# Moving small operations off VectorE in a fused attention and gated-unit kernel

## The chip, the cores and the metric

The kernel runs on one core of one Trainium2 chip. The metric is the device time of one execution in microseconds (us), lower is better. Before the change it is 220.66 us, the median of three runs (220.55 to 221.03). Times are compared by the ratio to the kernel before. Kernels are compared only within the same rounds. Line numbers such as L645 are lines of the kernel in question, so the same statement has another number before and after the change.

## The reference

The input x (2048 tokens of 512 channels, bfloat16) is layer-normalised to xn. Two branches of xn are added to x.

```python
qkv = xn @ wqkv                                   # 32 heads of 16
pq, pk = q @ w_phi, k @ w_phi                     # per head, 16x16
phi = concat([softmax(p), softmax(-p)])           # for q and for k: 32 features a head
kv  = sum_s phi_k[s] v[s]^T ;  z = sum_s phi_k[s]
A   = (phi_q kv) / (phi_q z + 1e-6) @ wo
B   = ((xn @ w_gate) * (xn @ w_up)) @ w_down      # width 1792
out = x + A + B
```

## The kernel before

All work is recorded as steps with their reads and writes. A small planner in the kernel's program orders the steps on each engine by assumed costs and issues them in that order, with semaphores between engines. TensorE has six PSUM banks in a ring for everything but two accumulators. Its matmuls are nearly all of the kernel's time; in the notes below a matmul of "512 columns" is one whose moving operand has 512 columns.

The parts that the change touches:

```python
# head: loads. SP is SyncE's queue, ACT is ScalarE's
load_x(SP, 0, 1)
load_x(ACT, 1, 1)                 # the second tile of 128 tokens, "x1"
load_gu(SP, "g", 0, 2)
load_gu(ACT, "u", 0, 2)
# ... cut ...
sc.chain("st0 ag0 st1 ag1 nm0 nm1 xe0d xe1d st2 ...")   # order forced on VectorE

def LN(ts, turn=True, ...):       # st = statistics, ag = their aggregate
    # ... bn_stats, bn_aggr on VectorE; Ln, Exp on ScalarE give rstd ...
    dve(tensor_scalar(out=xn, in0=x, scalar1=mean, scalar2=rstd, op0=subtract, op1=mult))
    # tiles 4 to 15 (turn=True) are then transposed by DMA, tiles 0 to 3 by TensorE

def even_up(ev, sm, rc, ratio, name, t):          # once per tile for k, once for q
    dve(tensor_tensor(out=ratio, in0=smv[:, :, 0], in1=rc, op=mult))      # 128x32, float32
    pool(tensor_tensor(out=ev1, in0=ev1, in1=ratio.broadcast, op=mult))   # GpSimd

def V(t):
    dve(tensor_tensor(out=o1, in0=psum_v, in1=rs.broadcast, op=mult))
    dve(tensor_copy(out=ve[:, :, 64:68], in_=rp_))                        # the cast, 128x32

def U(ft, sg):                    # a gated unit: two PSUM banks
    g = act(copy of bank bg)
    h = dve(tensor_tensor(out=h, in0=bank(bu), in1=g, op=mult))           # L710: frees the bank

def TSUMS():                      # sums of w_down blocks, on GpSimd, 128x1792 elements each
    sums(POOL, T1, ...); sums(POOL, T2, ...); sums(POOL, T4, ...); sums(POOL, T3, ...)
# ... cut: matmuls of the down projection, posts on VectorE, stores ...
```

The softmax here doesn't subtract the row's maximum and nothing guards it: scores larger than these inputs give would overflow.

## Time and profile before

| | before |
|---|---|
| time, median of 3 | 220.66 us |
| span of the profiled run | 219.2 us |
| busy: TensorE, VectorE, ScalarE, GpSimd | 211.1, 174.1, 80.4, 112.4 us |
| matmuls in the program, records of them in the trace | 1634, 1612 |

TensorE is busy 96% of the span. The question is what its few idle moments are. The list of waits of the kernel before, cut to matmuls and weight loads (engine, line, releaser, total us, times, longest):

```profile
PE ps L449 <- DVE arena L710: 1.6, 1, 1.6
PEld ps L449 <- DVE arena L574: 1.5, 2, 1.1
PEld ps L449 <- ACT arena L421: 1.0, 2, 0.7
PEld ps L449 <- DMA arena<-in_B_w_up_dram: 0.6, 1, 0.6
```

One wait of 1.6 us stands out; the others shown are at the head, but for 0.3 us. The table of stretches of the kernel before shows where it is (busy us of each engine, number of instructions in brackets):

```profile
core 0: us, PE busy (x) PEld busy (x) DVE busy (x) ACT busy (x) POOL busy (x), PEclk, DMA share, GB/s
40.00:45.00 5.00, 4.95 (x31) 2.39 (x31) 5.00 (x13) 2.24 (x6) 1.06 (x1) 1.00 0.98 317
...
60.00:65.00 5.00, 3.36 (x34) 2.04 (x34) 5.00 (x8) 3.28 (x7) 4.88 (x3) 1.00 0.00 0
65.00:70.00 5.00, 5.00 (x31) 2.41 (x30) 5.00 (x7) 1.62 (x4) 4.87 (x3) 1.00 0.00 0
```

VectorE has no free moment there (5.00 of 5 us), yet the number of its instructions falls from 13 to 7 per stretch once GpSimd is full too. The timeline at that place shows why (start, duration, engine, line, operation):

```profile
61.94 3.57 POOL L788 TENSOR_TENSOR arena<-arena 128x1792 bf16<-128x1792 bf16 x1
61.98 0.68 DVE L710 TENSOR_TENSOR arena<-ps,arena 128x512 bf16<-128x512 f32 x1
...
62.94 3.33 PE L449 MATMUL ps<-arena 128*128 128x512 bf16 x14 [1.64 <-DVE arena L710]
63.04 0.62 DVE L668 TENSOR_TENSOR arena<-ps,arena 128x512 bf16<-128x512 f32 x1
63.58 1.98 DVE L645 TENSOR_TENSOR arena<-arena 128x32 f32<-128x32 f32 x1
```

The ratio product L645 has 32 elements per partition and lasts 1.98 us. It ends at 65.56, when GpSimd's subtraction L788 ends (65.51). The product at 61.98, with one input in PSUM, runs under the same subtraction in its usual 0.68 us. The groups of the kernel before (busy us, mean ns of one; then idle time before):

```profile
L645 DVE TENSOR_TENSOR arena<-arena 128x32 f32<-128x32 f32 x32 | 17.3, 542 | 0.0
L671 DVE CAST arena<-arena 128x32 bf16<-128x32 f32 x16 | 6.7, 421 | 0.0
L574 DVE TENSOR_SCALAR arena<-arena 128x512 bf16<-128x512 bf16 x16 | 6.4, 429 | 0.3 <-ACT arena L421 0.3
```

The same shows all through this trace. Of the 32 ratio products 13 start while GpSimd runs a subtraction (L788). Each of these ends 0.045 to 0.049 us after that subtraction, and they last 0.28 to 1.98 us; the other 19 last 0.16 to 0.19 us, with a median of 0.18. Of the 16 casts (L671) six start with more than 0.1 us of a product or a subtraction of GpSimd (L647, L788) to go. They end 0.03 to 0.04 us after one and last 0.56 to 1.90 us; the other ten last 0.17. Two of the 16 normalisings (L574) are longer too, 0.77 and 0.67 us against 0.30 to 0.41, and end 0.15 us after a GpSimd instruction. The other groups of VectorE show none of it: the median of L710 is 675 ns for the 14 that start during a GpSimd product or subtraction and 673 for the 14 that meet none, and the reductions L639 take 1.22 us in both cases. Below, an instruction that ends in this way just behind one of GpSimd is said to wait it out.

### The profile page before, as it was taken

The page shows a single profiled execution, that of the slowest core. Times are in us where ns is not written, and L with a number is a line of the kernel's source. Part 1 is how long each engine was busy: PE and PEld are TensorE (multiplying, and loading weights), DVE is VectorE, ACT ScalarE, POOL GpSimd, SP SyncE. Part 2 cuts the span into 40 slices and gives each one's busy share as a digit, 9 for nine tenths or more (in the row PEclk, how much of TensorE's full clock was granted, in tenths as well). Part 3 has the DMA queues.
Part 4 walks back from the last instruction along what each step waited for, and adds up shares of the span by engine and source line. Part 5 has one row for each costly group of instructions (what it writes and reads, how often), then busy time and mean ns, then how long its engine had stood idle before and what let it go on. Part 6 is the DMA issues. An engine that isn't in the chain of part 4 may idle for free.

```text
span 219.2 us, 4090 instructions
## 1 busy us (share of the span) xinstructions
PE 211.1 (96%) x1612; PEld 139.7 (64%) x1634; DVE 174.1 (79%) x370; ACT 80.4 (37%) x173; POOL 112.4 (51%) x88
## 2 busy tenths in 40 slices
PE   8989999999979999999999999999999999999994
PEld 2775444444534454455565667888888888888983
DVE  3856999999999999699994748766877599667652
ACT  3647554354463334536432322333142332341000
POOL 5300031129899896256717535838658567311630
PEclk9999999999999999999999999999999999999998
DMA  6999872762200000002573040341453504535221
GB/s 187 312 253 377 193 145 51 238 174 90 51 0 0 3 0 0 0 4 48 96 98 74 30 89 3 84 110 41 95 60 72 99 24 99 95 72 89 57 75 49
DMA packets 48019, 19.95 MB, mean 91 GB/s; under 512 B 36848, under 2 KB 48000, under 8 KB 48000
## 3 DMA queue, kind: packets, MB, share of 16 engines
q1 hardware_dynamic: 47296, 19.28, 38.5%
q10 hardware_dynamic: 672, 0.39, 0.6%
q8 instruction: 13, 0.21, 0.4%
q14 instruction: 6, 0.05, 0.1%
q0 software_dynamic: 32, 0.02, 0.1%
HBM read 8.67 MB, written 2.10 MB: 49 GB/s over the span
## 4 chain that ended last, share of the span: by engine, by line
PE 73%; DVE 16%; DMA 5%; issue 4%; ACT 1%; SPq 1%
PE ps L449 73%; DVE arena L639 3%; DMA arena<-in_B_w_up_dram 3%; DVE arena L710 2%; DVE arena L566 2%; DMA arena<-arena 2%; DVE arena L657 2%; DVE arena L574 2%; DVE arena L668 2%; DVE arena L671 1%; DVE arena L645 1%; ACT arena L421 1%; SPq L172 1%; DVE arena L822 0%; DVE arena L568 0%
## 5 line engine op out<-in xcount | busy, mean ns | idle before, releaser
L449 PE MATMUL ps<-arena 128*128 128x256 bf16 (+3 forms) x1602 | 206.7, 289 | 4.1 <-DVE arena L710 1.6
L449 PEld LDWEIGHTS ps<-arena 128*128 128x128 bf16 x1624 | 138.3, 98 | 73.1 <-DVE arena L710 1.6
L421 ACT ACTIVATE arena<-ps 128x512 bf16<-128x512 f32 (+2 forms) x152 | 75.3, 535 | 117.2 <-PE ps L449 116.2
L788 POOL TENSOR_TENSOR arena<-arena 128x896 bf16<-128x896 bf16 (+1 forms) x36 | 74.4, 2070 | 38.8 <-PE ps L449 28.3
L647 POOL TENSOR_TENSOR arena<-arena 128x512 bf16<-128x512 bf16 x32 | 33.9, 1059 | 54.8 <-DVE arena L645 53.3
L639 DVE TENSOR_REDUCE arena<-arena 128x64 f32<-128x1024 bf16 x32 | 38.7, 1210 | 8.8 <-ACT arena L421 8.8
L822 DVE TENSOR_TENSOR arena<-ps,arena 128x256 f32<-128x256 f32 (+1 forms) x64 | 26.2, 415 | 11.7 <-PE ps L449 11.3
L710 DVE TENSOR_TENSOR arena<-ps,arena 128x512 bf16<-128x512 f32 x38 | 25.4, 669 | 5.9 <-PE ps L449 5.7
L721 DVE TENSOR_TENSOR arena<-ps,arena 128x256 bf16<-128x256 f32 x34 | 14.0, 412 | 10.3 <-ACT arena L421 10.3
L645 DVE TENSOR_TENSOR arena<-arena 128x32 f32<-128x32 f32 x32 | 17.3, 542 | 0.0
L566 DVE BATCH_NORM_STATS2 arena<-arena 128x6 f32<-128x512 bf16 x16 | 10.3, 671 | 2.5 <-DMA arena<-in_A_x_dram 2.5
L769 DVE TENSOR_TENSOR arena<-ps,arena 128x512 bf16<-128x512 f32 x16 | 11.0, 687 | 0.4
L668 DVE TENSOR_TENSOR arena<-ps,arena 128x512 bf16<-128x512 f32 x16 | 10.2, 637 | 0.4 <-PE ps L449 0.4
L657 DVE RECIPROCAL arena<-arena 128x64 f32<-128x64 f32 x16 | 8.6, 537 | 0.0
L421 ACT ACTIVATE arena<-arena 128x2 f32<-128x2 f32 (+1 forms) x20 | 5.0, 252 | 4.7 <-DVE arena L568 4.4
L671 DVE CAST arena<-arena 128x32 bf16<-128x32 f32 x16 | 6.7, 421 | 0.0
L574 DVE TENSOR_SCALAR arena<-arena 128x512 bf16<-128x512 bf16 x16 | 6.4, 429 | 0.3 <-ACT arena L421 0.3
L765 DVE RECIPROCAL arena<-arena 128x32 f32<-128x32 f32 x16 | 5.6, 347 | 0.3
L745 DVE RECIPROCAL arena<-arena 128x32 f32<-128x32 f32 x16 | 5.5, 344 | 0.1
L887 PE MATMUL ps<-const-bfloat16-1.0 128*128 128x512 bf16 x10 | 4.4, 629 | 0.8 <-PEq L1032 0.8
L549 POOL TENSOR_TENSOR arena<-arena 128x128 bf16<-128x128 bf16 x4 | 1.7, 426 | 3.4 <-DMA arena<-in_A_w_phi_dram 3.4
L887 PEld LDWEIGHTS ps<-const-bfloat16-1.0 128*128 128x128 bf16 x10 | 1.4, 142 | 3.0 <-issue 3.0
(17 smaller groups left out, 13.8 us busy)
## 6 DMA issues: line engine op xcount, KB each, us to landing
out_dram<-arena SPq DMA_DIRECT2D x15, 128.0 KB, 1.8
arena<-in_B_w_down_dram SPq DMA_DIRECT2D x1, 1792.0 KB, 7.9
arena<-in_A_x_dram SPq DMA_DIRECT2D x3, 512.0 KB, 10.4
arena<-in_B_w_gate_dram SPq DMA_DIRECT2D x1, 768.0 KB, 8.0
arena<-in_B_w_up_dram SPq DMA_DIRECT2D x1, 768.0 KB, 9.5
arena<-arena SPq DMA_TRANSPOSE x44, 3.0
arena<-in_B_w_gate_dram SPq DMA_DIRECT2D x2, 256.0 KB, 4.6
arena<-in_B_w_gate_dram SPq DMA_DIRECT2D x1, 512.0 KB, 7.1
```

The source lines that it names most:

```text
L421: return e.activation(out=out_ap, in_=in_ap, func=func, scale=scale, **kw)
L449: ins = e.matmul(o, lhsT=l, rhs=r, start=s, stop=p, skip_group_check=True)
L566: dve(lambda e, t=t: e.bn_stats(stats_v[:, t, :], x_tile(t)), [x_tile(t)], [stats_v[:, t, :]], cost=560.0, name=f"st{t}", win=win)
L639: dve(lambda e: e.tensor_reduce(out=sm, in_=Et.rearrange("p (h f) -> p h f", f=16), axis=AX.X, op=ALU.add), [Et], [sm], cost=1130.0, name= ...
L645: dve(lambda e: e.tensor_tensor(out=ratio, in0=smv[:, :, 0], in1=rc, op=ALU.mult), [sm, rc], [ratio], cost=100.0, name=f"{name}q{t}")
L647: pool(lambda e: e.tensor_tensor(out=ev[:, :, 1, :], in0=ev[:, :, 1, :], in1=ratio[:, :, None].to_broadcast([128, H, 16]), op=ALU.mult), [ ...
L657: dve(lambda e: e.reciprocal(out=rs, in_=sm), [sm], [rs], cost=500.0, name=f"kc{t}")
L668: dve(lambda e: e.tensor_tensor(out=o1, in0=src, in1=rp_[:, :, :, None].to_broadcast([128, 8, 4, 16]), op=ALU.mult), [src, rs_v[:, t % 4, ...
L710: dve(lambda e: e.tensor_tensor(out=h, in0=bank(bu), in1=g, op=ALU.mult), [bank(bu), g], [h], name=f"h{ft}.{sg}")
L721: dve(lambda e: e.tensor_tensor(out=h, in0=bank(b, 256, 256), in1=g, op=ALU.mult), [bank(b, 256, 256), g], [h], name=f"h{ft}.{s_lo}")
L788: fn = lambda e: e.tensor_tensor(out=out_, in0=a_, in1=b_, op=op)
L822: dve(lambda e: e.tensor_tensor(out=out_, in0=in_ps, in1=in_sb, op=ALU.add), [in_ps, in_sb], [out_], cost=328.0, name=f"{name}.{p}")
```

## The change

The intent is to take off VectorE what was seen to wait out GpSimd's instructions: the ratio goes to GpSimd, the normalising of tiles 4 to 15 and the casts to ScalarE. Around this, the loads of the head are re-ordered, w_phi is loaded through SyncE's queue, GpSimd's long sums are cut in quarters, tile 0 is normalised in two halves, two of the first 256-column units are cut into four of 128 columns, and the last stores are cut in quarters.

```diff
-    load_x(ACT, 1, 1)
+    load_x(SP, 1, 1)
     load_gu(SP, "g", 0, 2)
-    load_gu(ACT, "u", 0, 2)
+    load_gu(ACT, "u", 0, 2, after=identity)
@@ LN: tiles 4 to 15
-            dve(tensor_scalar(out=xn_tile(t), in0=x_tile(t), scalar1=mean, scalar2=rstd, ...))
+                pool(tensor_scalar(out=nb, in0=mean, scalar1=rstd, scalar2=-1.0, op0=mult, op1=mult))
+                act_op(xn_tile(t), x_tile(t), func=Identity, scale=rstd, bias=nb)
@@ even_up
-        dve(lambda e: e.tensor_tensor(out=ratio, in0=smv[:, :, 0], in1=rc, op=ALU.mult), ...)
+        pool(lambda e: e.tensor_tensor(out=ratio, in0=smv[:, :, 0], in1=rc, op=ALU.mult), ...)
@@ V
-        dve(lambda e: e.tensor_copy(out=ve[:, :, 64:68], in_=rp_), ...)
+        sc.step(ACT, lambda e: e.activation(out=ve[:, :, 64:68], in_=rp_, func=ACTF.Copy), ...)
@@ TSUMS: each of the four sums
+            for lo, hi in ((0, 2), (2, 4), (4, 6), (6, HF)):
+                sums(POOL, o_[:, lo:hi], a_[:, lo:hi], b_[:, lo:hi], ALU.subtract, ...)
@@ last pair of tiles: three quarter stores by SP as soon as each is ready, and
+                store(t2, 256, 256, ACT)
@@ head
-    for ft in range(4): U2(ft, 256)
+    U1(0, 2); U1(1, 2); U1(0, 3); U1(1, 3); U2(2, 256); U2(3, 256)
-    sc.chain("st0 ag0 st1 ag1 nm0 nm1 xe0d ...")
+    sc.chain("st0 ag0 st1 ag1 nm0.0 nm0.1 nm1 xe0d ...")
(cut: the moved w_phi load, allocation of nb, helpers)
```

More of the change, by code (lines that the diff above doesn't have):

```diff
@@ L388, in _build @@
     alloc("eps", 2 * 2)
+    alloc("nb", 2 * NT)
     alloc("sums", 2 * 4 * 64)
@@ L505, in load_sq @@
         return sc.dma(eng, v, src, nbytes, writes=[v], name=name, after=after)
+    identity = pool(lambda e: e.memset(ident, 0.0), [], [ident], 150.0, name="c")
     load_x(SP, 0, 1)
-    load_x(ACT, 1, 1)
+    load_x(SP, 1, 1)
     load_gu(SP, "g", 0, 2)
-    load_gu(ACT, "u", 0, 2)
+    load_gu(ACT, "u", 0, 2, after=identity)
     sc.step(ACT, lambda e: e.preload_act_table_set("natural_log_exp_and_others"), cost=1300.0, lat=0.0, name="tbl")
@@ L516, in _build @@
     load_gu(SP, "u", 4, 4)
+    sc.dma(SP, wphi_v, bass.AP(tensor=A_w_phi.tensor, offset=A_w_phi.offset, ap=[[16, 128], [2048, NQ], [1, 16]]),
+           16384, writes=[wphi_v], name="wphi")
     load_wT(1)
@@ L523, in _build @@
     load_x(SP, 12, 4)
-    sc.chain("x0 wg0 x2 wg2 wu2 wg4 wu4 wT1 wv x4 wg8 wu8 x8 x12")
-    sc.chain("x1 wu0 tbl")
-    def ms_fn(e):
-        return e.memset(ident, 0.0)
-    pool(ms_fn, [], [ident], 150.0, name="c")
+    sc.chain("x0 x1 wg0 x2 wg2 wu2 wg4 wu4 wphi wT1 wv x4 wg8 wu8 x8 x12")
+    sc.chain("wu0 tbl")
     def af_fn(e):
@@ L534, in _build @@
     pool(af_fn, [ident], [ident], 250.0, name="c")
-    sc.dma(POOL, wphi_v, bass.AP(tensor=A_w_phi.tensor, offset=A_w_phi.offset, ap=[[16, 128], [2048, NQ], [1, 16]]),
-           16384, writes=[wphi_v], name="wphi")
     def band(ap, nb, w, blk):
@@ L558, in _build @@
     eps_f = sbf("eps", 0, 1)
+    nb_v = sbf("nb", 0, NT)
     dve(lambda e: e.memset(eps_f, 1e-5), [], [eps_f], cost=70.0, name="eps")
@@ L562, in xn_tile, with LN @@
         return sbv("xn", (t % 4) * 512, 512)
-    def LN(ts, turn=True, win=60.0, aevac=False):
+    def LN(ts, turn=True, win=60.0, halves=((0, 512),)):
         for t in ts:
@@ L573, in LN @@
         for t in ts:
-            dve(lambda e, t=t: e.tensor_scalar(out=xn_tile(t), in0=x_tile(t), scalar1=mv_v[:, t, 0:1],
-                                               scalar2=rstd_v[:, t:t + 1], op0=ALU.subtract, op1=ALU.mult),
-                [x_tile(t), mv_v[:, t, :], rstd_v[:, t:t + 1]], [xn_tile(t)], cost=325.0, name=f"nm{t}", win=win)
             if turn:
+                pool(lambda e, t=t: e.tensor_scalar(out=nb_v[:, t:t + 1], in0=mv_v[:, t, 0:1],
+                                                    scalar1=rstd_v[:, t:t + 1], scalar2=-1.0, op0=ALU.mult,
+                                                    op1=ALU.mult),
+                     [mv_v[:, t, :], rstd_v[:, t:t + 1]], [nb_v[:, t:t + 1]], 150.0, name=f"nb{t}")
+                act_op(xn_tile(t), x_tile(t), func=ACTF.Identity, scale=rstd_v[:, t:t + 1], bias=nb_v[:, t:t + 1],
+                       name=f"nm{t}")
                 o = xnT_v[:, :, t * 128:(t + 1) * 128]
                 sc.dma(SP, o, xn_tile(t), 131072, turn=True, reads=[xn_tile(t)], writes=[o], name=f"xT{t}")
+                continue
+            for lo, n in halves:
+                dve(lambda e, t=t, lo=lo, n=n: e.tensor_scalar(out=xn_tile(t)[:, lo:lo + n], in0=x_tile(t)[:, lo:lo + n],
+                                                               scalar1=mv_v[:, t, 0:1], scalar2=rstd_v[:, t:t + 1],
+                                                               op0=ALU.subtract, op1=ALU.mult),
+                    [x_tile(t), mv_v[:, t, :], rstd_v[:, t:t + 1]], [xn_tile(t)[:, lo:lo + n]],
+                    cost=65.0 + 0.51 * n, name=f"nm{t}" if n == 512 else f"nm{t}.{lo // 256}", win=win)
     rp = [0]
@@ L644, in even_up @@
         smv = sm.rearrange("p (h s) -> p h s", s=2)
-        dve(lambda e: e.tensor_tensor(out=ratio, in0=smv[:, :, 0], in1=rc, op=ALU.mult), [sm, rc], [ratio],
-            cost=100.0, name=f"{name}q{t}")
+        pool(lambda e: e.tensor_tensor(out=ratio, in0=smv[:, :, 0], in1=rc, op=ALU.mult), [sm, rc], [ratio],
+             180.0, name=f"{name}q{t}")
         pool(lambda e: e.tensor_tensor(out=ev[:, :, 1, :], in0=ev[:, :, 1, :],
@@ L670, in V @@
             cost=600.0, name=f"vs{t}")
-        dve(lambda e: e.tensor_copy(out=ve[:, :, 64:68], in_=rp_), [rs_v[:, t % 4, :]],
-            [ve[:, c, 64:68] for c in range(8)], cost=90.0, name=f"vz{t}")
+        sc.step(ACT, lambda e: e.activation(out=ve[:, :, 64:68], in_=rp_, func=ACTF.Copy), reads=[rs_v[:, t % 4, :]],
+                writes=[ve[:, c, 64:68] for c in range(8)], cost=140.0, name=f"vz{t}")
     def kvb(c):
@@ L784, in parts @@
     def parts(v):
-        return [v[:, k, :] for k in range(HF)]
+        return [v[:, k, :] for k in range(v.shape[1])]
     def sums(eng, out_, a_, b_, op, name):
@@ L795, in TSUMS @@
     def TSUMS():
-        sums(POOL, T1, B12, B11, ALU.subtract, "T1")
-        sums(POOL, T2, B22, T1, ALU.subtract, "T2")
-        sums(POOL, T4, B21, T2, ALU.subtract, "T4")
-        sums(POOL, T3, B22, B12, ALU.subtract, "T3")
+        for n, (o_, a_, b_) in enumerate(((T1, B12, B11), (T2, B22, T1), (T4, B21, T2), (T3, B22, B12))):
+            for lo, hi in ((0, 2), (2, 4), (4, 6), (6, HF)):
+                sums(POOL, o_[:, lo:hi], a_[:, lo:hi], b_[:, lo:hi], ALU.subtract, f"Ts{n}.{lo}")
     def hA(half, t):
@@ L823, in post, with store @@
             cost=328.0, name=f"{name}.{p}")
-    def store(t, lo, n):
+    def store(t, lo, n, eng=SP):
         o = sbv("ostg", (t % 4) * 512 + lo, n)
-        sc.dma(SP, out_flat[t * 128:(t + 1) * 128, lo:lo + n], o, n * 256, is_out=True, reads=[o],
+        sc.dma(eng, out_flat[t * 128:(t + 1) * 128, lo:lo + n], o, n * 256, is_out=True, reads=[o],
                name=f"out{t}.{lo}")
@@ L861, in s5 @@
             post(p, o(t2, 0), pb, t21, "c21")
+            if p == NT // 2 - 1:
+                store(t2, 0, 256)
         def s6():
@@ L865, in s6 @@
             post(p, o(t1, 1), pa, x(t1, 1), "c12")
+            if p == NT // 2 - 1:
+                store(t1, 256, 256)
         def s7():
@@ L869, in s7 @@
             post(p, o(t1, 0), pb, t11, "c11")
-            store(t1, 0, 512)
+            store(t1, 0, 256 if p == NT // 2 - 1 else 512)
         def s8():
@@ L876, in s8 @@
             if p == NT // 2 - 1:
-                store(t2, 0, 256)
-                store(t2, 256, 256)
+                store(t2, 256, 256, ACT)
             else:
@@ L891, in _build @@
     WARM(10)
-    LN([0], turn=False)
+    LN([0], turn=False, halves=((0, 256), (256, 256)))
     T(0, split=True)
@@ L905, in _build @@
     U2(3, 0)
-    for ft in range(4):
-        U2(ft, 256)
-    sc.chain("st0 ag0 st1 ag1 nm0 nm1 xe0d xe1d st2 ag2 st3 ag3 nm2 h0t0 nm3 xe2d h1t0 xe3d h0t1 h1t1")
-    sc.chain("ln0 rs0 ln1 rs1 xe0a xe1a ge0t0 ln2 rs2 ge1t0 ln3 rs3 ge0t1 xe2a ge1t1 xe3a")
+    U1(0, 2)
+    U1(1, 2)
+    U1(0, 3)
+    U1(1, 3)
+    U2(2, 256)
+    U2(3, 256)
+    sc.chain("st0 ag0 st1 ag1 nm0.0 nm0.1 nm1 xe0d xe1d st2 ag2 h0t0 st3 nm2 ag3 xe2d nm3 h1t0 h0t1 xe3d h1t1")
+    sc.chain("ln0 rs0 ln1 rs1 xe0a xe1a ge0t0 ge1t0 ln2 rs2 ge0t1 ln3 rs3 ge1t1 xe2a xe3a")
     units = [(U, ft, 0) for ft in range(4, NF)] + [(U, ft, sg) for sg in (1, 2) for ft in range(NF)]
```

## The prediction

> **What bounds the kernel now.** TensorE. The page has it busy 96% of the span. [...]I find 203.3 us of necessary time in 215.2 us between first and last matmul. The 11.8 us of excess are: about 2 us in the ten warm-up matmuls; four waits at the head (0.64 us before the first transpose, 0.36 at 5.8, 0.57 at 8.4 for the second w_up slice, landing at 8.93, and 0.69 at 11.1 for the evacuation of a transpose); some eighteen evenly spaced gaps of 0.22 us that answer to no wait; 0.30 at 115.8 for a transposing DMA; and one real stall, 1.81 us at 61.1, for VectorE (the product at L710 that frees a PSUM bank). After the last matmul come about 3.1 us of adds and stores.
>
> VectorE (79%) is full only from 24 to 80 us (window table: 5.00 of every 5 us). The chain of waits runs through it from 23 to 63 us, but that is backlog: TensorE keeps its full rate there, fed from six PSUM banks, until the backlog reaches it at 61.
>
> **What the change does.** The ratio product (L645) is 128x32; it takes 0.18 us when free, 542 ns on average, 1.98 us at 63.6 under a GpSimd subtraction. The cast at L671 averages 421 ns, free 0.17. [...] Taken off VectorE: 17.3 us of ratios, 6.7 of casts, 12 of 16 normalisings at 0.43 = 5.2; about 29 us, so 174 falls to about 145.
> Added: [...] GpSimd: 32 ratios and 12 small biases, estimate 0.2 us each: 112 to about 118.
>
> **On the critical path.** Per K tile VectorE's work falls from about 5.6 us to about 4.2, against about 4.5 of TensorE's: no backlog, so the stall at 61 goes (-1.8). After 63 us TensorE hardly waits for anything, so the other freed VectorE time is worth nothing. Head: the 0.69 us wait should nearly vanish (128-column units stand after the transposes: -0.5); the wait for w_up stays, perhaps +0.1 to +0.3 later, because x1 is now issued ahead of it by SyncE. Tail: three quarter stores leave earlier, the last through ScalarE's queue: -0.3. New stall: at 21 to 27 us ScalarE is already 4.0 of 5 us busy and gets four normalisings; expected 0.2. Sum: 220.7 - 1.8 - 0.5 - 0.3 + 0.2 + 0.2 = 218.4 us.
>
> **Range.** 217.2 to 219.6. Faster by over 2% (under 216.3): 4%; within 2%: 95%; slower: 1%.
>
> **Right if:** L710's stall at 61 is gone; VectorE near 145 us and no longer 5.00 of 5 in 25-60; matmul groups unchanged; w_up still ends a wait near 9 us; the chain runs through TensorE.
>
> **Wrong if:** ScalarE's normalisings delay the exponentials so that TensorE waits for a bank at 22-30 us; the ratio on GpSimd queues behind subtractions and delays query transposes, so that TensorE waits after 80 us; the w_up slice lands much later; or the 0.22 us gaps change.

The term of -1.8 us needs only the lengths that the trace shows. The 203.3 us of necessary time come out of the trace as well, to 0.5 us: with the median spacings in it (216, 109, 56 and 33 ns for 512, 256, 128 and 68 columns) the recorded matmuls take 203.8 us. The 0.2 us for a small GpSimd instruction is an estimate that names no figure.

## More of the kernel before

The head of the kernel before, in the timeline:

```profile
0.80 0.41 ACTq L172 DMA_DIRECT2D arena<-in_A_x_dram  x1
...
4.25 0.66 DVE L566 BATCH_NORM_STATS2 arena<-arena 128x6 f32<-128x512 bf16 x1
...
5.05 0.38 DVE L574 TENSOR_SCALAR arena<-arena 128x512 bf16<-128x512 bf16 x1
...
5.49 3.09 PE L449 MATMUL ps<-arena 128*128 128x128 bf16 x40 [0.22 <-DVE arena L574]
```

Ten warm-up matmuls occupy TensorE from 0.84 to 5.26 us; the first transpose starts at 5.49. The statistics of x1 (the line at 4.25) follow those of x0 without a wait for their load. In what follows, "the clock" is the one that TensorE is granted: in this trace 512-column matmuls start 427 ns apart (median) before 6.48 us, which is called half rate here, and 216 ns apart after it, the full rate.

## The result, and the profile after

The changed kernel takes 219.53 us (median of 4 runs, 219.14 to 219.87) against 220.75 us for the kernel before in the same comparison. The ratio of the two is 0.9943 with a 95% interval of 0.9922 to 0.9964. All ratios here are the mean time of one kernel's runs over the mean of the other's in the same rounds, so not quite the ratio of the medians quoted beside them. The range of the prediction holds the time, but the gain is half of the forecast 2.2 us. A second look at the same kernel (a_again below) gave a ratio of 0.9879 (0.9838 to 0.9921), a gain of about 2.7 us, so the size of the gain depends on the executions that one happens to draw; the head, below, is the likely reason.

The groups of the kernel after that answer to those of before:

```profile
L653 POOL TENSOR_TENSOR arena<-arena 128x32 f32<-128x32 f32 x32 | 8.3, 261 | 32.3 <-DVE arena L753 18.7
L679 ACT ACTIVATE arena<-arena 128x32 bf16<-128x32 f32 x16 | 3.7, 231 | 9.3 <-DVE arena L665 9.3
L422 ACT ACTIVATE arena<-arena 128x512 bf16<-128x512 bf16 x12 | 9.1, 805 | 1.4 <-POOL arena L573 1.4
```

Two stretches of the kernel after, the one where a new wait was feared and the one where TensorE had waited:

```profile
core 0: us, PE busy (x) PEld busy (x) DVE busy (x) ACT busy (x) POOL busy (x), PEclk, DMA share, GB/s
25.00:30.00 5.00, 5.00 (x25) 2.25 (x23) 3.54 (x8) 5.00 (x13) 0.94 (x4) 1.00 0.39 79
...
60.00:65.00 5.00, 5.00 (x43) 2.91 (x42) 2.79 (x5) 3.51 (x8) 5.00 (x6) 1.00 0.00 0
```

VectorE fell from 5.00 to 2.79 us in the stretch from 60 to 65, and TensorE's wait is gone. ScalarE is full from 25 to 30, but TensorE does not wait for it. In the chain that ended last, TensorE's share rose from 73% to 95% of the span (before, then after):

```profile
PE 73%; DVE 16%; DMA 5%; issue 4%; ACT 1%; SPq 1%
PE 95%; DMA 2%; DVE 1%; ACT 0%; SPq 0%; issue 0%
```

The head got worse. The timeline of the kernel after:

```profile
0.81 0.86 SPq L172 DMA_DIRECT2D arena<-in_A_x_dram  x2
...
2.97 0.69 DVE L564 BATCH_NORM_STATS2 arena<-arena 128x6 f32<-128x512 bf16 x1 [2.04 <-DMA arena<-in_A_x_dram]
...
4.84 0.69 DVE L564 BATCH_NORM_STATS2 arena<-arena 128x6 f32<-128x512 bf16 x1 [0.96 <-DMA arena<-in_A_x_dram]
...
5.66 1.10 DVE L583 TENSOR_SCALAR arena<-arena 128x256 bf16<-128x256 bf16 x3
...
6.04 11.19 PE L450 MATMUL ps<-arena 128*128 128x128 bf16 x114 [0.78 <-DVE arena L583]
```

x0 lands earlier than before (2.95 instead of 3.40), but x1, now second in SyncE's queue, lands only at 4.81 instead of 3.61. Its issue starts just 0.45 us later (1.25 instead of 0.80). What also changed is the order: ScalarE's queue, freed of x1, now issues the first slice of w_up (256 KB, twice x1) at 1.03, ahead of x1, where it was issued behind it before (1.24). That slice lands at 4.60, and x1 0.2 us after it. The two transfers were issued by different engines and yet ran at the same time: the packets of x1 lie at 3.3 to 4.3 us, among those of w_up (2.3 to 4.1). How much of the delay is the issue and how much is w_up was not separated. VectorE's forced order puts the statistics of x1 ahead of the normalising of x0, so everything waits for x1, and the first transpose starts 0.55 us later. That is not all. The stretches of one us just behind it, before:

```profile
7.00:8.00 1.00, 1.00 (x22) 1.00 (x20) 0.97 (x4) 0.29 (x2) 0.67 (x3) 1.00 1.15 324
```

and after:

```profile
7.00:8.00 1.00, 1.00 (x12) 0.96 (x11) 0.69 (x3) 0.38 (x1) 0.00 (x0) 1.00 1.13 306
8.00:9.00 1.00, 1.00 (x12) 1.00 (x11) 0.96 (x4) 0.28 (x1) 0.00 (x0) 1.00 1.09 354
```

The same 128-column matmuls run at half the rate: 12 instead of 22 begin in a us. In the trace they start 107 ns apart (median) in place of 56. The trace's clock events have the clock come up at 6.48 us before and at 10.07 us after. The page's column PEclk says 1.00 all along: it knows nothing ahead of the first event.

The difference of the two profiled spans is 1.65 us (219.23 and 217.58). Where it came from can be read off at fixed places of TensorE's program. The table gives the start (us) of the same group of 68-column matmuls, with the same columns ahead of it in both programs, and the two ends:

| place | before | after | difference | step |
|---|---|---|---|---|
| second group | 43.43 | 44.54 | +1.11 | head: +1.11 |
| seventh group | 68.04 | 67.43 | -0.61 | wait at 61: -1.72 |
| seventeenth group | 105.79 | 105.18 | -0.61 | 0 |
| twentieth group | 121.28 | 120.23 | -1.05 | small waits, one for a transposing DMA: -0.44 |
| last group | 206.89 | 205.84 | -1.05 | 0 |
| end of the span | 219.23 | 217.58 | -1.65 | stores: -0.60 |

This compares one execution of each. The other traces show how far two of the steps can be trusted. In the seven traces with the head of before, the second group starts between 42.97 (b_onein) and 44.03 us (b_rvz). From the seventeenth to the twentieth group the traces of all kernels take 15.05 to 15.60 us; c_x1warm, which has all of the freeing, takes 15.46, and b_onein, which moves nothing off VectorE, 15.05. So the -0.44 is not shown to come from the change. The step at 61 us is clear of this: from the sixth to the seventh group it is 8.05 us before and 8.07 in b_tail, and 6.32 or 6.33 in every trace with all of VectorE's freeing.

### The profile page after: what moved, and what is told of

It reads as the page before. It is cut to its first block, busy times and chain, and to the rows that moved or that the text cites. A ratio compares the mean times of both kernels' runs of the same rounds, so it can differ in the third digit from the quotient of the medians.

```text
span 217.6 us, 4184 instructions
## 1 busy us (share of the span) xinstructions
PE 213.3 (98%) x1650; PEld 141.4 (65%) x1650; DVE 152.7 (70%) x313; ACT 91.2 (42%) x203; POOL 123.3 (57%) x143
## 4 chain that ended last, share of the span: by engine, by line
PE 95%; DMA 2%; DVE 1%; ACT 0%; SPq 0%; issue 0%
PE ps L450 95%; DMA arena<-in_A_x_dram 2%; DVE arena L829 0%; DVE arena L564 0%; ACT arena L422 0%; DVE arena L583 0%; SPq L172 0%; DVE arena L566 0%
## 5 line engine op out<-in xcount | busy, mean ns | idle before, releaser
L450 PE MATMUL ps<-arena 128*128 128x256 bf16 (+3 forms) x1640 | 208.8, 291 | 0.9 <-DVE arena L583 0.8
L450 PEld LDWEIGHTS ps<-arena 128*128 128x128 bf16 x1640 | 140.0, 99 | 70.4 <-DVE arena L583 2.3
L796 POOL TENSOR_TENSOR arena<-arena 128x896 bf16<-128x896 bf16 (+2 forms) x48 | 76.4, 1600 | 25.8 <-PE ps L450 16.7
L829 DVE TENSOR_TENSOR arena<-ps,arena 128x256 f32<-128x256 f32 (+1 forms) x64 | 26.4, 414 | 11.8 <-PE ps L450 11.6
L653 POOL TENSOR_TENSOR arena<-arena 128x32 f32<-128x32 f32 x32 | 8.3, 261 | 32.3 <-DVE arena L753 18.7
L729 DVE TENSOR_TENSOR arena<-ps,arena 128x256 bf16<-128x256 f32 x32 | 13.2, 414 | 11.7 <-ACT arena L422 11.7
L422 ACT ACTIVATE arena<-arena 128x2 f32<-128x2 f32 (+2 forms) x32 | 14.0, 457 | 4.5 <-DVE arena L566 2.7
L573 POOL TENSOR_SCALAR arena<-arena 128x1 f32<-128x1 f32 x12 | 3.0, 265 | 17.0 <-ACT arena L422 17.0
L679 ACT ACTIVATE arena<-arena 128x32 bf16<-128x32 f32 x16 | 3.7, 231 | 9.3 <-DVE arena L665 9.3
```

What stands on the lines that cost most here:

```text
L422: return e.activation(out=out_ap, in_=in_ap, func=func, scale=scale, **kw)
L450: ins = e.matmul(o, lhsT=l, rhs=r, start=s, stop=p, skip_group_check=True)
L729: dve(lambda e: e.tensor_tensor(out=h, in0=bank(b, 256, 256), in1=g, op=ALU.mult), [bank(b, 256, 256), g], [h], name=f"h{ft}.{s_lo}")
L796: fn = lambda e: e.tensor_tensor(out=out_, in0=a_, in1=b_, op=op)
L829: dve(lambda e: e.tensor_tensor(out=out_, in0=in_ps, in1=in_sb, op=ALU.add), [in_ps, in_sb], [out_], cost=328.0, name=f"{name}.{p}")
```

## The experiments

"On before" means the kernel before plus the edit shown, "on after" the changed kernel plus the edit. The ratio is to the kernel before. By the measurement's rule of 2% only b_ratio differs (slower); the differences below that are read from the intervals and the profiles. The whole list first:

| run | kernel | median us | lowest to highest | ratio (95% interval) |
|---|---|---|---|---|
| b_all3 | before + VectorE freed | 219.04 | 218.35 to 221.13 | 0.9934 (0.9896 to 0.9973) |
| b_onein | before, ratio as an op with one SBUF input | 220.13 | 219.84 to 220.63 | 0.9966 (0.9948 to 0.9985) |
| b_ratio | before, ratio on GpSimd | 228.85 | 228.81 to 229.59 | 1.0368 (1.0344 to 1.0392) |
| b_rvz | b_ratio, casts on ScalarE | 219.24 | 218.68 to 220.62 | 0.9922 (0.9881 to 0.9964) |
| b_rts | b_ratio, sums in quarters | 222.15 | 220.75 to 222.74 | 1.0035 (0.9995 to 1.0076) |
| b_tail | before, last stores in quarters | 220.41 | 220.00 to 221.02 | 0.9965 (0.9935 to 0.9995) |
| a_x1act | after, x1 by ScalarE's queue | 217.97 | 217.61 to 218.15 | 0.9867 (0.9845 to 0.9888) |
| a_warm13 | after, 13 warm-ups | 218.11 | 217.83 to 219.47 | 0.9872 (0.9841 to 0.9904) |
| a_again | after, unaltered | 218.50 | 217.88 to 219.53 | 0.9879 (0.9838 to 0.9921) |
| c_x1warm | a_x1act, 12 warm-ups | 218.29 | 217.95 to 218.48 | 0.9861 (0.9822 to 0.9899) |
| c_t0first | after, tile 0 first | 218.95 | 218.78 to 219.54 | 0.9897 (0.9862 to 0.9933) |
| c_x1cool | a_x1act, 8 warm-ups | 218.67 | 217.37 to 219.30 | 0.9887 (0.9854 to 0.9919) |

### b_all3: the freeing of VectorE alone

On before: the hunks LN, even_up, V and TSUMS of the diff above; the loads, the head and the stores stay.

> The kernel before with only the freeing of VectorE (ratio on GpSimd, normalising of tiles 4 to 15 and the casts on ScalarE, weight sums in quarters); head, load order and stores as before. Theory: the freeing alone removes the 1.8 us wait of TensorE at 61 us and up to 0.3 us near 116, the first 512-column matmul stays near 15.4 us, and the tail after the last matmul stays 3.1 us: 218.7 to 219.0 us, which is less than the whole change takes (219.5). Rival: the gain of the whole change came from head and tail, and the wait at 61 only moved to another place: 220.2 us or more.

Measured 219.04 us. The profiled span is 217.4 us; the second 68-column group starts at 43.41 (before 43.43), the seventh at 66.30 (before 68.04). So the head did not move and the wait at 61 us went: -1.74 us at that place, all of it from freeing VectorE. The rival is out. The stretch that shows it:

```profile
60.00:65.00 5.00, 5.00 (x43) 2.89 (x42) 2.80 (x5) 3.64 (x8) 5.00 (x7) 1.00 0.00 0
```

The median is 0.04 us above the expected window. Two runs of six (220.57, 221.13) are slower, and no profile was taken of them. The record does list their granted clock, though: 0.992 and 0.991, where the other four have 1.0. A share of 0.992 over 218 us is about 3.5 us at half clock, which would cost about 1.7 us (estimates from these two figures). Where in the kernel it lay is not known. Three of the four slowest runs of the kernel before (222.50, 222.90 and 223.02) have 0.992 too.

### b_onein: is it the second SBUF input?

On before, in place and order unchanged (the sum over one element copies the sum instead of forming the ratio; the comparison with the reference let it pass within its tolerance). Its output is wrong, which doesn't matter for the time.

```diff
-  dve(tensor_tensor(out=ratio, in0=smv[:, :, 0], in1=rc, op=mult), ...)
+  dve(tensor_reduce(out=ratio, in_=smv[:, :, 0:1], axis=X, op=add), ...)
```

> The kernel before with the ratio product replaced, on VectorE in the same place and with the same waits, by a sum over one element, which reads one SBUF tensor (wrong result on purpose). [...]the 32 instructions take below 0.25 us on average instead of 542 ns, with none over 0.4, VectorE's busy time falls by about 10 us, and the wait at 61 us shrinks below 0.4 us: 218.9 to 219.4 us. Rival (the long times are the wait for the result of the reciprocal just before, or time of the instruction itself): mean stays above 0.45 us and the time at 220.4 or more.

(The theory as it was tested: the ratio product is long because of its second SBUF input.)

The groups of this run:

```profile
L645 DVE TENSOR_REDUCE arena<-arena 128x32 f32<-128x32 f32 x32 | 5.5, 173 | 0.0
L671 DVE CAST arena<-arena 128x32 bf16<-128x32 f32 x16 | 9.9, 616 | 0.0
```

With the same waits and one SBUF input, the instruction takes 173 ns instead of 542, and none of the 32 over 186. So the long times were not the wait for the reciprocal in front of it, nor a small instruction's own time. The edit changes the operation along with the number of inputs, so it does not show which of the two counts. In the kernel before, the product at 61.98, with one of its two inputs in PSUM, runs through the same subtraction unlengthened, but six of the casts, with one input in all, wait a GpSimd instruction out. And the cast behind it went up from 421 to 616 ns, VectorE's busy time fell by 7.3 us (to 166.8) rather than 10, and TensorE's wait at 61 us shrank only from 1.6 to 1.1 us. The gain was 0.6 us, less than I expected. Part of the waiting had only moved to the cast.

### b_ratio, b_rvz, b_rts: the ratio on GpSimd, alone and in company

On before: b_ratio has only the hunk even_up; b_rvz has even_up and V; b_rts has even_up and TSUMS.

> The kernel before with only the ratio moved to GpSimd. If any part of the freeing is enough to keep the backlog from reaching TensorE at 61 us: 218.8 to 219.3 us, wait at 61 below 0.4 us, and the casts still slow (mean 0.35 us or more). If all three parts are needed: 219.8 us or more.

> The kernel before with the ratio on GpSimd and the casts on ScalarE; normalising on VectorE and the weight sums whole (3.6 us each). Theory: [...]without it VectorE has nothing left that meets the long sums but a few normalisings: no TensorE wait over 0.5 us between 50 and 80 us, 218.8 to 219.5 us. Rival: the whole weight sums in front of the ratio in GpSimd's queue were the trouble: TensorE still waits several us there, 223 us or more.

> The kernel before with the ratio on GpSimd and the weight sums in quarters (1.1 us at most); casts and normalising stay on VectorE. Theory (the cast takes the wait, for as long as the GpSimd instruction it meets): the cast's mean falls from 1469 ns to between 500 and 900, TensorE's waits at 50 to 75 us shrink but do not all go, 219.3 to 222 us. [...]other rival (the casts play no part): below 219.2.

b_ratio is 8 us slower than the kernel before. The first branch of the expectation was a gain of about 1.7; the second, 219.8 us or more, holds the result only because it had no upper end, and I had not foreseen a loss. The timelines of its GpSimd and VectorE:

```profile
62.59 0.27 POOL L645 TENSOR_TENSOR arena<-arena 128x32 f32<-128x32 f32 x1 [2.30 <-DVE arena L657]
62.81 3.57 POOL L788 TENSOR_TENSOR arena<-arena 128x1792 bf16<-128x1792 bf16 x1
```

```profile
61.98 0.54 DVE L657 RECIPROCAL arena<-arena 128x64 f32<-128x64 f32 x1
62.44 0.62 DVE L668 TENSOR_TENSOR arena<-ps,arena 128x512 bf16<-128x512 f32 x1
62.98 3.44 DVE L671 CAST arena<-arena 128x32 bf16<-128x32 f32 x1
```

GpSimd waits for the reciprocal, does the ratio in 0.27 us, and at once starts a subtraction of 3.57 us. VectorE reaches its cast 0.17 us after that and waits it out: the cast ends at 66.42 us, the subtraction at 66.38. The same pattern repeats at 56.15 and 69.07. The move has tied the start of GpSimd's longest instruction to the moment just ahead of VectorE's cast:

```profile
L671 DVE CAST arena<-arena 128x32 bf16<-128x32 f32 x16 | 23.5, 1469 | 0.0
```

TensorE then waits (one wait for L710 is 4.2 us), it is busy for 1.80 us of the stretch from 65 to 70, and there and in the next its clock falls to a mean of 0.72 and 0.60 (PEclk in the stretches of this run):

```profile
65.00:70.00 5.00, 1.80 (x5) 0.70 (x6) 5.00 (x6) 0.32 (x1) 3.71 (x4) 0.72 0.01 2
70.00:75.00 5.00, 5.00 (x16) 1.83 (x15) 5.00 (x5) 1.68 (x3) 3.65 (x3) 0.60 0.00 0
```

The other two runs show which part of this is needed. With the cast on ScalarE as well (b_rvz) the time is 219.24 us, although the sums are still whole and the normalising is still on VectorE: in this run the whole sums (3.6 us each) do no harm that the time shows once the ratio and the cast are off VectorE. TensorE's wait at 61 us is all but gone (6.56 us from the sixth to the seventh 68-column group, 6.32 in b_all3). Its profiled run, at 219.75 us one of the two slow ones of four, has another wait, at 20 us:

```profile
19.98 0.69 DVE L566 BATCH_NORM_STATS2 arena<-arena 128x6 f32<-128x512 bf16 x1 [1.38 <-DMA arena<-in_A_x_dram]
20.59 0.68 DVE L710 TENSOR_TENSOR arena<-ps,arena 128x512 bf16<-128x512 f32 x1
...
21.32 6.86 PE L449 MATMUL ps<-arena 128*128 128x512 bf16 x30 [0.83 <-DVE arena L710]
```

The load of tile 4 came late, VectorE's statistics stood in front of a product that frees a bank, and TensorE waited 0.8 us: such a load can be one source of the spread. The slowest run, 220.62, has a granted clock of 0.992, like the two of b_all3. With the cast left and the sums in quarters (b_rts) the cast falls from 1469 to 670 ns and the time to 222.15 us, no better than before and just above the expectation. So the cast was what took over the waiting, and it waits longer the longer the GpSimd instructions are (quarters against whole sums). Moving the ratio without the cast is a loss of 3.7%; moving both is a gain of 0.8%.

b_rvz lacks the normalising on ScalarE and the quartered sums, and is within the noise of b_all3 (ratios 0.9922 and 0.9934). Those two moves gained nothing that the times resolve; at 61 us the two traces differ by 0.24 us (6.56 and 6.32).

### b_tail: the last stores

On before: the last hunk but one of the diff.

> The kernel before with only the last stores in quarters, the last through ScalarE's queue. Theory: the time from the last matmul's start to the span's end falls from 3.2 to 2.6 us, nothing else moves: 220.1 to 220.4 us against 220.7. Rival: the last landing is bound by the transfer itself and nothing is gained: 220.6 to 220.9.

Measured 220.41 us, ratio 0.9965. From the start of the last matmul to the end of the span it is 2.82 us, before 3.43: the 0.6 us are there. The median is 0.01 us above the expected window, and the interval of the ratio just excludes no gain.

### a_x1act, a_warm13, a_again, c_x1warm, c_x1cool: the head

On after. a_x1act:

```diff
-    load_x(SP, 1, 1)
+    load_x(ACT, 1, 1)
```

The order strings of the two queues change with it. a_warm13 changes `WARM(10)` to `WARM(13)`; a_again changes nothing; c_x1warm is a_x1act with `WARM(12)`, c_x1cool a_x1act with `WARM(8)`.

> The changed kernel with the second x tile loaded through ScalarE's queue again, as before. Theory: the new load order cost the head: x1 landed at 4.8 us instead of 3.6, the first transpose began at 6.04 instead of 5.49, and TensorE's clock then came up at 10.1 instead of 6.5 us. With x1 back: x1 lands near 3.6, the first transpose at 5.3 to 5.5, clock up at 6.5 to 7, first 512-column matmul near 15.2 instead of 16.6: 218.0 to 218.6 us. Rival (the head is later for another reason, such as the halved normalising or the w_phi load in SyncE's queue): first transpose still near 6 us and 219.3 us or more.

> The changed kernel (x1 still in SyncE's queue) with 13 instead of 10 warm-up matmuls, so that TensorE is not idle for 0.8 us before its first transpose. Theory: the idle stretch from 5.3 to 6.0 us is why the clock came up only at 10.1 us; without it the clock comes up at 5.5 to 7.5 us, the 32 first unit matmuls take 56 ns instead of 107, and the first 512-column matmul starts near 15.6 instead of 16.6 us: 218.4 to 219.0 us. Rival: the clock's rise falls at a moment of its own, whatever the gap; then it is spread from run to run, and the mean is 219.5 to 220.0 because the three warm-ups only push the transposes back.

> The changed kernel, unaltered, once more, for the moment at which TensorE's clock comes up and for the spread of its times. If the late rise (10.1 us) belongs to this kernel's head: clock up again at 9 to 11 us, or, when it comes up before 5.3 us as in the run with 13 warm-ups, a first 512-column matmul near 15.2 us and 218.0; so times in two clusters, near 218.0 and near 219.5, median 219.2 to 219.8. If the first look was a chance: all times between 218.0 and 218.6.

> The changed kernel with x1 through ScalarE's queue and 12 warm-ups. If the late clock is the whole of what both single edits won (218.0 and 218.1), the two together give no more: 217.7 to 218.2. If they win different things (the earlier load 0.6, the clock 1.0): 217.2 to 217.6.

> The changed kernel with x1 through ScalarE's queue (218.0 us in five of five runs) and only 8 warm-ups instead of 10, which opens the idle stretch before the first transpose from 0.6 to about 1.2 us while every load stays where it was. If an idle stretch of that length is what makes the clock come up late in some executions: times in two clusters, near 218.0 and near 219.3 to 219.6, at least two of six in the slow one, and where the profile falls in the slow one the clock rises at 9 to 11 us. If the load order itself is what costs: all six between 217.5 and 218.3.

a_x1act takes 217.97 us, all five runs between 217.61 and 218.15. x1 lands at 3.61 us, the first transpose starts at 5.45 and the clock comes up at 6.23. Its stretch from 7 to 8 us:

```profile
7.00:8.00 1.00, 1.00 (x22) 1.00 (x20) 0.96 (x5) 0.48 (x3) 0.00 (x0) 1.00 1.14 325
```

This undoes the loss of the head. It beats the kernel before and the first four runs of the changed kernel; the interval of its ratio (0.9845 to 0.9888) overlaps that of a_again, three of whose six runs are as fast. It does not yet tell whether the load or the clock is what costs.

a_warm13 keeps the late load. Its first transpose starts at 5.95 us, as late as in the changed kernel (6.04), but its matmuls run 56 ns apart from then on, and its second 68-column group starts at 43.03 us, 1.51 us sooner (44.54); a_x1act's starts at 42.78. So in these traces the clock is 1.51 of the 1.76 us. The reason I gave was not tested by that profile, though: the clock had come up at 4.1 us, during the warm-ups (their spacing falls from 427 to 220 ns there), and the idle stretch before the first transpose was still there:

```profile
5.95 0.54 PE L450 MATMUL ps<-arena 128*128 128x128 bf16 x4 [0.56 <-DVE arena L583]
```

Nor is it a sure cure: one of its six runs takes 219.47 us and one 218.65, and neither was profiled.

a_again shows that it is a matter of chance in the changed kernel: six runs fall into 217.88, 217.91, 218.07 and 218.94, 219.33, 219.53. The profiled one is the 219.53, and its clock came up at 10.18 us. The fast three left no profile, so that their clock came up earlier is inferred. The four runs of the first comparison (219.14 to 219.87) all lie with the slow ones, though two of them (219.66, 219.87) have a granted clock of 0.992, by the estimate above some 3.5 us at half clock, and may be slow by that and not by a late rise. c_x1warm (all six 217.95 to 218.48, the median 0.09 us above the window of the first branch) shows that the two cures together give no more than either (ratios 0.9861, 0.9867 and 0.9872), so both remove the same thing.

c_x1cool then opens the idle stretch again (1.27 us, where a_x1act has 0.19) while no load is re-ordered. The matmuls of its first 14 us:

```profile
0.84 3.57 PE L897 MATMUL ps<-const-bfloat16-1.0 128*128 128x512 bf16 x8 [0.84 <-PEq L1046]
5.68 8.49 PE L450 MATMUL ps<-arena 128*128 128x128 bf16 x84 [1.27 <-DVE arena L583]
```

The slow runs come back (219.10 and 219.30; the profiled one is the 219.10, clock up at 9.73 us), with x1 landing early (3.90 us; a_x1act 3.61). The load order is therefore not what costs by itself; as far as these runs show, it costs by leaving TensorE idle for longer ahead of the first transpose (0.78 us in the changed kernel, 0.19 in a_x1act), after which, in some executions, the clock comes up about 3.5 us later (9.73 us here, 6.23 in a_x1act). The other four runs (217.37 to 218.84) spread more than two clean groups would.

How long an idle stretch is too long is not shown. In the three traces with a late rise TensorE idles 0.78 us (the changed kernel), 0.87 (a_again) and 1.27 us (c_x1cool) between its warm-ups and the first transpose. With an idle stretch of 0.19 us (a_x1act), 0.22 (the kernel before), 0.26 (b_all3), 0.29 (b_onein) and 0.43 (b_ratio), behind ten warm-ups of the same 4.42 us, the 128-column matmuls run at full rate by 8 us at the latest. But b_tail has 0.86 us and a_warm13 0.56 and both are at full rate as well: there the warm-ups had already sped up ahead of the idle stretch (ten in 3.74 us, thirteen in 4.55). And a_again has fast and slow runs with one and the same head. So in these traces a late rise goes with 0.78 us or more of idleness behind warm-ups at half rate; what else decides it in an execution was not found.

### c_t0first: an attempt at a better head

On after: VectorE's order `st0 ag0 nm0.0 nm0.1 st1 ...`, ScalarE's `ln0 rs0 xe0a ln1 ...`, and the two units of tile 0 ahead of tile 1's transposes.

> The changed kernel with x1 in SyncE's queue, but tile 0 taken all the way first: normalised before tile 1's statistics, and its two units before tile 1's transposes. x0 lands at 2.95, x1 at 4.8 us: first transpose at 4.8 to 5.3, no idle stretch over 0.5 us before 9 us, clock up by 7.2 at the latest, w_up's slice at 8.2 us is the next wait: first 512-column matmul at 14.2 to 14.8, 217.2 to 217.9 us. Rival (only the queue of the load matters): 219 or more.

Missed: 218.95 us, nearly the rival's 219. The first transpose starts at 4.89 us as intended, but in this run TensorE then idles three times (matmuls of the first 14 us):

```profile
4.89 0.53 PE L450 MATMUL ps<-arena 128*128 128x128 bf16 x4
6.27 1.29 PE L450 MATMUL ps<-arena 128*128 128x128 bf16 x20 [0.84 <-ACT arena L422]
8.08 3.04 PE L450 MATMUL ps<-arena 128*128 128x128 bf16 x36 [0.52 <-ACT arena L422]
11.96 2.24 PE L450 MATMUL ps<-arena 128*128 128x128 bf16 x31 [0.84 <-DVE arena L583]
```

The forced orders made evacuations and normalisings wait behind each other. With x1 in SyncE's queue the head cannot be mended by order alone, or not by this one.

## Why the prediction was right or wrong

- **VectorE's backlog and the wait at 61 us: right.** I gave -1.8 us; -1.72 was measured at the fixed places, and b_all3 shows it with the freeing alone. VectorE is still full from 30 to 35 and from 40 to 45 us (5.00 of 5), against my "no longer 5.00 of 5 in 25-60"; from 50 us on it is not, and that is where it counted.
- **After 63 us nothing is gained: right as far as these runs tell.** In the two profiles 0.44 us of small waits between 105 and 121 us is gone, which I had not put into the sum; but that stretch varies by as much from trace to trace, with the change and without it, so it counts as luck.
- **Stores: right in kind, half in size.** -0.3 predicted, -0.60 measured, and b_tail finds the same 0.6 alone.
- **ScalarE's new stall: wrong, harmlessly.** ScalarE is full from 25 to 30 us, but TensorE does not wait; +0.2 predicted, 0 found.
- **The head: this step failed.** The prediction said: "the wait for w_up stays, perhaps +0.1 to +0.3 later, because x1 is now issued ahead of it by SyncE", and together with the 128-column units it made the head -0.3. In the first profile of the changed kernel it was +1.11 at the second 68-column group. I looked for the cost of the new queue in the transfer behind x1. That one came earlier (8.15 us against 8.93); x1 itself came 1.2 us later, with a later issue and w_up's first slice ahead of it, and through VectorE's forced order it held up even x0. And I did not think of the clock at all: with the longer idle stretch (0.78 us against 0.22) it came up at 10.07 instead of 6.48 us. a_x1act, a_warm13, a_again and c_x1cool show that this second part is most of the loss and that it strikes some executions and not others. In the fast ones the changed kernel takes 217.9 to 218.1 us, below my figure; in the slow ones 218.9 to 219.9.
- **The range held because errors of both signs met, which is luck.** In the two profiles the head cost 1.4 us more than predicted; stores, the small waits and ScalarE were 0.9 us better (0.30 + 0.44 + 0.20 = 0.94). My terms add up to 218.5, not 218.4.
- **A reading of the trace was wrong.** The "some eighteen evenly spaced gaps of 0.22 us that answer to no wait" are records that the trace lost. The kernel before has 1634 matmuls, and its trace has 1634 weight loads but only 1612 matmuls; the evenly spaced gaps have the length of one 512-column matmul, 216 ns. The first trace of the changed kernel is complete (1650 of both) and has no such gap; the trace of a_again misses 22 again, and each of the 13 traces whose records were counted (all but that of c_x1warm) is complete or lacks exactly 22, all of 512 columns. By the median spacings of the trace the necessary time is therefore about 208.6 and not 203.3 us (203.8 for the recorded matmuls, and 22 x 216 ns = 4.75 us more), and what could be won from TensorE's idleness was about 6.6 us of the 215.2, not 11.8 (estimates from these figures).
- **Busy times.** GpSimd rose to 123.3 us, not 118: 44 instructions of 0.2 us are 8.8 us and not 6, so my own figures gave 121; and the ratio and the bias take 261 and 265 ns. ScalarE came to 91.2 us, from 80.4; a normalising takes 805 ns there and a cast 231. VectorE fell to 152.7 us, not 145: neighbouring records overlap (63.04 + 0.62 against the next start, 63.58, is 0.08 us), and busy time counts an overlap once. The lengths of all its instructions add up to 196.1 us before and 168.2 after, 27.9 less; but 6.5 us of overlaps went with them, so the busy time fell by 21.4 only.

What stays open: in which stretch the runs with a granted clock near 0.992 (two of b_all3, one of b_rvz, two of the changed kernel) run at the lower clock, since none of them was profiled; whether the fast runs of the changed kernel do have an early clock; and what, besides the idle stretch, makes the clock come up late in some executions.

## What to carry to other kernels

When VectorE instructions end just behind those of GpSimd, list every group of VectorE in the trace that does so and move all the frequent ones together: moving one hands the wait to the next (the cast went from 421 to 616 ns in b_onein and to 1469 in b_ratio), and the engine that received it may start its own long instruction just ahead of that one (0.17 us ahead, in b_ratio). A load that is re-ordered at the head costs or gains by its own landing (x1 here, 1.2 us later), and by the order in which the engine behind it must take the tiles, before it does so by what stands behind it in the queue. TensorE's idle time ahead of its first real work is worth keeping short: here the three traces with a late clock had 0.78 to 1.27 us of it, and a_x1act, whose five runs were all fast, 0.19. A single profile of such a head says little: look at several runs and their granted clock, and count the records before calling a gap a wait.
